# Weight scales and k's column maxima by a GpSimd reduction over partitions, and batch 2's VectorE steps placed behind the splits of w_in

## The chip, the cores and the metric

The kernel runs on one core of a Trainium2 chip. The metric is the device time of one execution in microseconds. The kernel before has a median of 852.67 us over 3 runs (851.4 to 853.17). One further execution was recorded by the hardware profiler; all lines of a profile or trace below are of that one.

## The reference

An attention without a score matrix (q is normalized along its 64 elements, k along its 576 rows) feeds a feed-forward layer of two weights.

```python
# q, k, v: 8 batches x 8 heads x 576 rows x 64; x: 4608 tokens x 512
q_s = np.exp(q - np.max(q, axis=-1, keepdims=True))
q_s = q_s / (np.sum(q_s, axis=-1, keepdims=True) + 1e-09)
k_s = np.exp(k - np.max(k, axis=2, keepdims=True))
k_s = k_s / (np.sum(k_s, axis=2, keepdims=True) + 1e-09)
kv = np.einsum('bhsd,bhse->bhde', k_s, v)
x = np.einsum('bhsd,bhde->bhse', q_s, kv)        # tokens x 512
h = x @ w_in                                     # 512 -> 2048
sp = np.maximum(h, 0.0) + np.log1p(np.exp(-np.abs(h)))
out = (h * erf(sp)) @ w_out                      # 2048 -> 512
```

q, k and v are float32, the two weights are float64.

## The kernel before, in words

**Layout.** A batch has 576 rows: 512 of them lie on 128 partitions (four rows each, two tiles of four heads, `k_0` and `k_1`, `q_0` and `q_1`), the last 64 are a tail (`kt`, `qt`, `vtail`). Two batches form a pair, and a pair's 1152 tokens are three blocks of 384. The feed-forward layer takes a block in four groups of 512 hidden columns: that gives 48 items n, each with a first product (`m`, w_in), the activation (`T`, `G`, `U`) and a second product (`M`, w_out).

**Number formats.** Items 0 to 3 multiply in float32 (L1038, L1116). From item 4 on every operand is split into two float16 parts (hi on ScalarE by `ACTIVATE`, L297; lo on VectorE by `SCALAR_TENSOR_TENSOR`, L298). The first product then uses seven products of sums (`pX`, `pY`, `pZ`, L999), and these need sums of parts of w_in (L322); the second uses three (L1125). The splits scale each group of a weight by a power of two, found from the weight's squares: `wsquares` (Q) collects them on ScalarE, `wscales` (Z, L247 and on) takes the maxima and sets `w_s` (scales), `w_u` (their inverses), `GA`, `GB` and `VW`. `unit` (L1044) makes from `w_u` the factor U of a batch and group for batches 0 and 1.

**Weights.** They arrive as pairs of 32-bit words in sixteen pieces of 1 MB. `wload` issues the first eight through SyncE's queue and the others through GpSimd's:

```python
eng = nc.sync if i < LOADS.count("w") else nc.gpsimd
```

`wdecode` (D, L210 to L216, three VectorE operations for a half piece) turns a piece into float32 and calls `wload` for the next one. A piece's issue waits on its queue for its buffer.

**Maxima of k.** `k_max` (L497 to L501) leaves `kmax`, 128x512, the maxima over each partition's rows. What is still missing is the maximum over partitions. `k_max_T` transposes `kmax` on TensorE (four 128x128, tile `kT` in PSUM) and reduces it on VectorE (`km`, L512); `k_max_rows` transposes `km`'s columns, broadcast, back (`kB` in PSUM). VectorE then subtracts kB from `kt`, `k_0` and `k_1`. The scales of the weights are found in the same manner (`ws_in`, `ws_out`, L259).

**What sets the order.** The text `ORDER` lists the steps of the start and of items 0 to 3; `tok` runs one. Batch 0 has steps of its own in `start` (kmax, kT, kB, qm, ks, ke, qn, kv, ...), where q's second half is subtracted on GpSimd (L871). Batch 1 runs through the generator `attention` and the later ones through `attention16`, one stage at each `A`. From item 4 on a loop lists the steps, `SPLITS` names the weights to split behind an item (S a split, R w_in's sums), and `pace` takes as many `A` as the share of the work done calls for. A scheduler then places the listed operations on each engine's queue, by when it takes their operands to be ready; every engine runs its queue in order. The functions that the change touches:

Of the kernel before, what the change touches and what calls it, by code (L numbers as in the profile page):

```python
# [9 lines left out]
F32 = mybir.dt.float32  # L10
# [23 lines left out]
    kmax qm0 kT kB qe0 qm1 ks2 ks0 ks1 ke2 ke0 ke1 qn0 t0 t1 qe1 qn1 w6 kv0 kn0 kv1 kn1  # L34
# [8 lines left out]
SPLITS = {4: "S2 S3 R3", 5: "S4 S5 R5", 6: "S6", 7: "S7"}  # L43

OUT32 = range(0)
# [12 lines left out]
def attn_moe_kernel(  # L58
# [89 lines left out]
    GB = small[:, 32:36]  # L148
# [100 lines left out]
    def wscales():  # L249


        assert len(wsq) == NJ
        nc.vector.tensor_reduce(small[:, 24:32], sq4, axis=AX.X, op=ALU.max)
        for i, (which, e2) in enumerate((("in", 52), ("out", 50))):

            bk = psh.tile([P, 512], F32, tag="pY" if i == 0 else "pZ", name=f"ws_{which}")
            for g in range(NG):
                o = 24 + 4 * i + g
                nc.tensor.transpose(  # L259
                    bk[:, g * P:(g + 1) * P], small[:, o:o + 1].to_broadcast([P, P]), ident  # L260
                )
            e = at.tile([P, NG], F32, tag="wse", name=f"wse_{which}")
            nc.vector.tensor_reduce(
                e, bk.rearrange("p (g s) -> p g s", g=NG), axis=AX.X, op=ALU.max
            )
            nc.vector.tensor_scalar_max(e, e, TINY)
            nc.vector.tensor_scalar(
                e.bitcast(I32), e.bitcast(I32), 24, 23,
                op0=ALU.logical_shift_right, op1=ALU.logical_shift_left,
            )  # L270
            nc.vector.reciprocal(w_s[which], e)
            nc.vector.tensor_scalar_mul(w_s[which], w_s[which], 2.0**-e2)
            nc.vector.tensor_scalar_mul(w_u[which], e, 2.0**e2)
        wready.add("all")
        m = at.tile([P, 4], F32, tag="wm", bufs=1, name="wm")
        for n, (w, op) in enumerate(
            ((w_s["in"], ALU.min), (w_s["out"], ALU.min),
             (w_u["in"], ALU.max), (w_u["out"], ALU.max))
        ):
            nc.vector.tensor_reduce(m[:, n:n + 1], w, axis=AX.X, op=op)  # L280
        nc.vector.tensor_scalar(
            GA, w_u["out"], m[:, 0:1], m[:, 1:2], op0=ALU.mult, op1=ALU.mult
        )
        nc.vector.scalar_tensor_tensor(
            GA, GA, 2.0**-20, w_u["in"], op0=ALU.mult, op1=ALU.mult
        )
# [4 lines left out]
        nc.vector.tensor_scalar(
            GB, w_u["in"], m[:, 0:1], m[:, 1:2], op0=ALU.mult, op1=ALU.mult
        )
        nc.vector.tensor_scalar_mul(GB, GB, 2.0**-20)

    def split2(src, hi, lo, s):
        nc.scalar.activation(hi, src, AF.Copy, scale=s)  # L297
        nc.vector.scalar_tensor_tensor(lo, src, s, hi, op0=ALU.mult, op1=ALU.subtract)  # L298

    def wsplit(jn):  # L300
# [7 lines left out]
        if which == "out":  # L308
            split2(stg.pop(jn), whalf(jn, 0), whalf(jn, 1), s)
            wdone(jn)  # L310
            return
# [12 lines left out]
    def wsplit_sums(jn):  # L324
        which, g = wjobs[jn]
        sg = stg.pop(jn).rearrange("p (c f) -> p c f", c=4)
        for i in range(2):
            hi, lo = (
                wop(jn, h, 3 + 2 * i, 2).rearrange("p n c f -> p (n c) f") for h in range(2)
            )  # L330
            split2(sg[:, :, 256 * i:256 * i + 256], hi, lo, w_s[which][:, g:g + 1])
        wdone(jn)
# [184 lines left out]
    def k_max_rows(b, km):  # L517

        bk = bank(f"kB_{b}")
        for c in range(NC4):  # L520
            nc.tensor.transpose(
                bk[:, c * P:(c + 1) * P], km[:, c:c + 1].to_broadcast([P, P]), ident
            )
        return bk.rearrange("p (h d) -> p h d", h=H)

# [204 lines left out]
    def attention(b):  # L730
# [96 lines left out]
    def start():  # L827
# [58 lines left out]
        def put(key, val):  # L886
            r[key] = val

        def tc_(c):
# [19 lines left out]
            "kT": ("kmax", lambda: put("km", k_max_T(0, r["kmax"]))),  # L909
            "kB": ("kT", lambda: put("kb", k_max_rows(0, r["km"]))),  # L910
# [162 lines left out]
    def gmul(n):  # L1073
        s, g = st[n], seq[n][2]
        if n < NG:
# [27 lines left out]
    def mm2(n, tt):  # L1103
# [9 lines left out]
        if n < NG or n in OUT32:  # L1113
# [38 lines left out]
    def tok(name):  # L1152
# [71 lines left out]
    for n in range(4, N + 2):  # L1224
# [51 lines left out]
```

## Time and profile before

| | before |
|---|---|
| median of 3 runs | 852.67 us (851.4 to 853.17) |
| the profiled execution | 853.86 us, of which the span (first to last instruction) 851.7 us |
| granted TensorE clock, mean | 0.988 |
| TensorE busy | 811.2 us, 6448 matmuls |
| VectorE busy | 638.2 us, 913 instructions |
| ScalarE busy | 503.0 us, 633 instructions |
| GpSimd busy | 17.6 us, 37 instructions |

PE is TensorE, PEld its weight loads, DVE VectorE, ACT ScalarE, POOL GpSimd, SP SyncE. A row of the timeline has the start in us from the span's start, the duration in us, the engine, the line of the kernel, the operation, the tiles (out<-in) and their size; in brackets stands the time that the engine stood idle before it and what ended this. A row of the windows gives for each stretch of time its length, the busy time of each engine with the number of instructions, the granted clock, the share of time in which the DMA engines were busy, and GB/s.

### The profile page before, as it was taken

The page shows a single profiled execution, that of the slowest core. Times are in us where ns is not written, and L with a number is a line of the kernel's source. Part 1 is how long each engine was busy: PE and PEld are TensorE (multiplying, and loading weights), DVE is VectorE, ACT ScalarE, POOL GpSimd, SP SyncE. Part 2 cuts the span into 40 slices and gives each one's busy share as a digit, 9 for nine tenths or more (in the row PEclk, how much of TensorE's full clock was granted, in tenths as well). Part 3 has the DMA queues.
Part 4 walks back from the last instruction along what each step waited for, and adds up shares of the span by engine and source line. Part 5 has one row for each costly group of instructions (what it writes and reads, how often), then busy time and mean ns, then how long its engine had stood idle before and what let it go on. Part 6 is the DMA issues. An engine that isn't in the chain of part 4 may idle for free.

```text
span 851.7 us, 15370 instructions
## 1 busy us (share of the span) xinstructions
PE 811.2 (95%) x6448; PEld 553.8 (65%) x6448; DVE 638.2 (75%) x913; ACT 503.0 (59%) x633; POOL 17.6 (2%) x37
## 2 busy tenths in 40 slices
PE   2999998899999999999999999999999999999997
PEld 1655557567667667766776676766776676777673
DVE  5999899998997879758865779748866657554543
ACT  2598486777564556555673566555663565543532
POOL 2010000000000000000000000000000000000000
PEclk8899999899999999999999999999999999999999
DMA  9997420016416402412134302322121000100100
GB/s 255 407 250 197 120 75 13 1 25 112 106 35 131 108 9 61 103 31 51 51 70 98 87 14 51 93 51 51 38 51 38 38 2 1 38 1 1 38 1 37
DMA packets 145508, 62.59 MB, mean 73 GB/s; under 512 B 134688, under 2 KB 136736, under 8 KB 145440
## 3 DMA queue, kind: packets, MB, share of 16 engines
q1 hardware_dynamic: 143264, 53.23, 25.1%
q0 software_dynamic: 2176, 8.39, 2.8%
q8 instruction: 50, 0.82, 0.4%
q14 instruction: 18, 0.15, 0.1%
HBM read 45.09 MB, written 9.44 MB: 64 GB/s over the span
## 4 chain that ended last, share of the span: by engine, by line
PE 64%; DVE 19%; ACT 10%; issue 3%; SPq 2%; DMA 1%; ACTq 0%; POOL 0%; DVEq 0%
PE o L1125 27%; PE pX L999 15%; PE pZ L999 7%; ACT G L344 4%; PE o L1116 4%; ACT L344 3%; PE pY L999 3%; DVE G L1079 3%; PE kv L542 2%; DVE H L1097 2%; PE pX L1038 2%; DVE H L1093 2%; SPq L409 2%; PE x L632 1%; DVE wi L298 1%
## 5 line engine op out<-in xcount | busy, mean ns | idle before, releaser
L1125 PE MATMUL o<-wo,H 128*128 128x512 f16 x1584 | 367.0, 380 | 2.8 <-DVE H L1093 1.8
L999 PEld LDWEIGHTS <-wi 128*128 128x128 f16 x3696 | 311.2, 98 | 44.3 <-issue 15.7
L1125 PEld LDWEIGHTS <-H 128*128 128x128 f16 x1584 | 152.7, 98 | 157.4 <-DVE H L1093 2.6
L999 PE MATMUL pX<-x,wi 128*128 128x192 f16 x2112 | 206.2, 248 | 7.6 <-ACT H L1018 4.5
L344 ACT ACT_TABLE_LOAD x104 | 133.4, 1283 | 2.8 <-DVE H L1024 0.8
L1079 DVE SCALAR_TENSOR_TENSOR G<-G,small,H 128x1536 f32<-128x1536 f32 x44 | 79.9, 1817 | 56.2 <-ACT G L344 56.0
L1026 ACT COPY H<-pX 128x384 f32<-128x384 f32 x44 | 20.9, 475 | 165.3 <-PE pX L999 159.9
L999 PE MATMUL pZ<-x,wi 128*128 128x192 f16 x1056 | 104.0, 247 | 3.4 <-ACT x L297 1.8
L344 ACT ACTIVATE G<-H,U 128x768 f32<-128x768 f32 (+1 forms) x60 | 72.7, 1231 | 22.1 <-DVE H L1024 21.5
L1097 DVE TENSOR_TENSOR H<-G,H 128x1536 f16<-128x1536 f32 x44 | 77.2, 1755 | 1.0
L344 ACT ACTIVATE G<-G 128x1536 f32<-128x1536 f32 x48 | 71.2, 1484 | 0.5
L999 PE MATMUL pY<-x,wi 128*128 128x192 f16 x528 | 51.9, 247 | 0.0
L1024 DVE TENSOR_TENSOR H<-pZ,H 128x384 f32<-128x384 f32 x44 | 24.4, 554 | 32.5 <-PE pZ L999 32.1
L1011 DVE COPY H<-pY 128x384 f32<-128x384 f32 x44 | 24.3, 553 | 30.3 <-PE pY L999 30.3
L1116 PE MATMUL o<-wo,G 128*128 128x512 f32 x96 | 43.4, 597 | 0.0
L1093 DVE CAST H<-G 128x1536 f16<-128x1536 f32 x44 | 42.1, 957 | 0.8
L297 ACT ACTIVATE x<-x 128x768 f16<-128x768 f32 (+1 forms) x44 | 32.9, 763 | 12.8 <-DVE x L388 11.1
L1141 DVE TENSOR_SCALAR ob<-o,V 128x512 f32<-128x512 f32 x29 | 21.7, 748 | 24.5 <-PE o L1125 24.5
L298 DVE SCALAR_TENSOR_TENSOR x<-x,x 128x768 f16<-128x768 f32 (+1 forms) x44 | 37.0, 851 | 3.2 <-ACT x L297 3.2
L1013 DVE TENSOR_TENSOR H<-pX,H 128x384 f32<-128x384 f32 x44 | 24.4, 554 | 15.9 <-PE pX L999 15.7
L443 ACT ACTIVATE x<-x 128x384 f32<-128x384 f32 (+1 forms) x52 | 17.5, 394 | 30.0 <-PE x L632 27.4
L1116 PEld LDWEIGHTS o<-wo,G 128*128 128x128 f32 x96 | 17.5, 190 | 18.7 <-issue 18.2
(184 smaller groups left out, 762.7 us busy)
## 6 DMA issues: line engine op xcount, KB each, us to landing
out_dram<-ob SPq DMA_DIRECT2D x32, 256.0 KB, 2.4
vbuf<-in_v_dram SPq DMA_DIRECT2D x60, 128.0 KB, 3.1
q<-in_q_dram SPq DMA_DIRECT2D x56, 128.0 KB, 3.4
k<-in_k_dram SPq DMA_DIRECT2D x56, 128.0 KB, 3.1
wo<-in_moe_w_in_dram SPq DMA_DIRECT2D x4, 1024.0 KB, 17.2
wi<-in_moe_w_out_dram POOLq DMA_DIRECT2D x2, 1024.0 KB, 8.9
wi<-in_moe_w_in_dram SPq DMA_DIRECT2D x2, 1024.0 KB, 9.4
raw<-in_moe_w_out_dram POOLq DMA_DIRECT2D x2, 1024.0 KB, 8.0
```

The lines of the kernel that those rows point to most:

```text
L297: nc.scalar.activation(hi, src, AF.Copy, scale=s)
L298: nc.vector.scalar_tensor_tensor(lo, src, s, hi, op0=ALU.mult, op1=ALU.subtract)
L344: i = nc.scalar.activation(out_, in_, func, **kw)
L999: nc.tensor.matmul(o, w[wl][:, c, a * P:(a + 1) * P], x[:, xl, xi, c, :], start=(new and a == 0 and c == 0 and i == 0), stop=(c == 1 and i ...
L1011: nc.vector.tensor_copy(C[0, 0], bank2("Y"))
L1013: add(C[0, 0], bank2("X"), C[0, 0], op=ALU.add)
L1024: add(C[0, 1], bank2("Z"), C[0, 1], op=ALU.add)
L1079: nc.vector.scalar_tensor_tensor(flat(s["G"]), flat(s["G"]), (GB if n in OUT32 else GA)[:, g:g + 1], flat(s["H"]), op0=ALU.mult, op1=ALU.mult,
L1093: nc.vector.tensor_copy(flat(s["gh"]), flat(s["G"]))
L1097: nc.vector.tensor_tensor(flat(s["gl"]), flat(s["G"]), flat(s["gh"]), op=ALU.subtract)
L1116: nc.tensor.matmul(o, s["G"][:, a, ts_], w[:, a, :], start=(first_ and a == 0), stop=(last_ and a == FG - 1),)
L1125: nc.tensor.matmul(o, s[gt][:, a, ts_], w[wl][:, a, :], start=(first_ and a == 0 and i == 0), stop=(last_ and a == FG - 1 and i == 2),)
```

## The change

- **k's maxima of batches 0 and 1.** `k_max_all` takes the place of `k_max_T` and `k_max_rows`: one `partition_all_reduce` on GpSimd takes `kmax` (128x512) and leaves in every partition of `kB`, now an SBUF tile, the maximum over the partitions. Later batches keep the way over TensorE. In `ORDER` the steps kT and kB become one, kB, directly behind kmax.
- **The weights' scales.** `wscales` takes the eight columns of both weights through one `partition_all_reduce` (128x8), and computes scales and inverses of both at once. `GB` goes; `unit` makes the four factors of a batch in one operation.
- **The order behind the splits.** `wsplit` keeps in `wlast` the last lo split of the latest group of w_in; attention's stages and the splits of w_out are issued behind that instruction (`tc.issue_after`). In `SPLITS` the splits of w_out come behind those of w_in.
- `OUT32`, which was empty, and the branches that asked for it are gone.

```diff
 ORDER = """
-    kmax qm0 kT kB qe0 qm1 ks2 ks0 ks1 ke2 ke0 ke1 qn0 t0 t1 qe1 qn1 w6 kv0 kn0 kv1 kn1
+    kmax kB qm0 qe0 qm1 ks2 ks0 ks1 ke2 ke0 ke1 qn0 t0 t1 qe1 qn1 w6 kv0 kn0 kv1 kn1
...
-SPLITS = {4: "S2 S3 R3", 5: "S4 S5 R5", 6: "S6", 7: "S7"}
+SPLITS = {4: "S3 R3 S2", 5: "S5 R5 S4", 6: "S6", 7: "S7"}
...
         nc.vector.tensor_reduce(small[:, 24:32], sq4, axis=AX.X, op=ALU.max)
-        for i, (which, e2) in enumerate((("in", 52), ("out", 50))):
-
-            bk = psh.tile([P, 512], F32, tag="pY" if i == 0 else "pZ", name=f"ws_{which}")
-            for g in range(NG):
...
-            nc.vector.tensor_scalar_mul(w_u[which], e, 2.0**e2)
+        e = small[:, 32:40]
+        nc.gpsimd.partition_all_reduce(e, small[:, 24:32], P, bass_isa.ReduceOp.max)
+        nc.vector.tensor_scalar_max(e, e, TINY)
+        nc.vector.tensor_scalar(
+            e.bitcast(I32), e.bitcast(I32), 24, 23,
+            op0=ALU.logical_shift_right, op1=ALU.logical_shift_left,
+        )
+        nc.vector.tensor_scalar_mul(w_u["in"], e[:, :NG], 2.0**52)
+        nc.vector.tensor_scalar_mul(w_u["out"], e[:, NG:], 2.0**50)
+        nc.vector.reciprocal(small[:, 4:12], small[:, 12:20])
...
-        for n, (w, op) in enumerate(
-            ((w_s["in"], ALU.min), (w_s["out"], ALU.min),
-             (w_u["in"], ALU.max), (w_u["out"], ALU.max))
-        ):
-            nc.vector.tensor_reduce(m[:, n:n + 1], w, axis=AX.X, op=op)
+        for n, (c, op) in enumerate(((4, ALU.min), (12, ALU.max))):
+            nc.vector.tensor_reduce(
+                m[:, 2 * n:2 * n + 2], small[:, c:c + 8].rearrange("p (w g) -> p w g", w=2),
+                axis=AX.X, op=op,
+            )
...
+    wlast = [None]
+
+    def behind(ins):
+
+        return tc.issue_after(ins) if ins is not None else nullcontext()
...
         if which == "out":
-            split2(stg.pop(jn), whalf(jn, 0), whalf(jn, 1), s)
+            with behind(wlast[0]):
+                split2(stg.pop(jn), whalf(jn, 0), whalf(jn, 1), s)
...
-            split2(sg[:, :, 256 * i:256 * i + 256], hi, lo, w_s[which][:, g:g + 1])
+            r = split2(sg[:, :, 256 * i:256 * i + 256], hi, lo, w_s[which][:, g:g + 1])
+        wlast[0] = r.ins
...
+    def k_max_all(b, kmax):
+
+        kb = at.tile([P, DM], F32, tag="qT", name=f"kB_{b}")
+        nc.gpsimd.partition_all_reduce(kb, hd(kmax), P, bass_isa.ReduceOp.max)
+        return kb.rearrange("p (h d) -> p h d", h=H)
...
-        km = k_max_T(b, kmax)
+        kb = k_max_all(b, kmax)
         q_sub(rows(qs[0]), 16, f"q_{b}_0")
         yield SHARES[1]
-        kb = k_max_rows(b, km)
...
-            "kT": ("kmax", lambda: put("km", k_max_T(0, r["kmax"]))),
-            "kB": ("kT", lambda: put("kb", k_max_rows(0, r["km"]))),
+            "kB": ("kmax", lambda: put("kb", k_max_all(0, r["kmax"]))),
...
-        if b < 2 and (b, g) not in udone:
-            udone.add((b, g))
-            nc.vector.tensor_tensor(U, w_u["in"][:, g:g + 1], bat[b]["ux"], op=ALU.mult)
+        if b < 2 and b not in udone:
+            udone.add(b)
+            nc.vector.tensor_scalar_mul(bat[b]["U"], w_u["in"], bat[b]["ux"])
...
         if c == "A":
-            r = next(att, None)
+            with behind(wlast[0]):
+                r = next(att, None)
```

Three places show what the scheduler makes of it. First GpSimd's queue at the start. Before, behind the memsets of v's tail, it holds the issue of a piece of w_out (the buffer `wi_89`), q's second half and more issues:

```order
L433 MEMSET vtail 64x520
L434 MEMSET vtail 64x8
L189 DMA wi_89<-in_moe_w_out_dram 128x2x1024
L871 TENSOR_TENSOR q_1_136<-G_raw_1_109,q_1_m 128x1024
L433 MEMSET vtail 64x520
L434 MEMSET vtail 64x8
L189 DMA raw_359<-in_moe_w_out_dram 128x2x1024
L189 DMA wo_95<-in_moe_w_in_dram 128x2x1024
```

In the changed kernel the reduction stands there, between two `ISA` rows without operands (each loads a GpSimd library: the one for the reduction, then the one from before):

```order
L425 MEMSET vtail 64x520
L426 MEMSET vtail 64x8
L521 ISA
L521 ISA kB_146<-kmax_139 128x512
L868 ISA
L868 TENSOR_TENSOR q_1_136<-G_raw_1_109,q_1_m 128x1024
L425 MEMSET vtail 64x520
L426 MEMSET vtail 64x8
L188 DMA wi_89<-in_moe_w_out_dram 128x2x1024
L188 DMA raw_349<-in_moe_w_out_dram 128x2x1024
```

The issue of `wi_89` has moved from ahead of q's subtraction to behind it and behind the memset of the second v tail.

Second, VectorE's queue at the start, behind the last step of kmax. Before, `km` and q's maxima, then k's subtractions ahead of q's norm (`q_0_r`, L461 to L467):

```order
L501 TENSOR_TENSOR kmax_139<-kmax_139,kt_105 64x512
L512 TENSOR_REDUCE km_154<-kT_149 128x4
L870 TENSOR_REDUCE q_0_m<-H_raw_q 128x16
L857 TENSOR_TENSOR kt_105<-kt_105,kB_156 64x512
L871 TENSOR_TENSOR q_0_135<-H_raw_q,q_0_m 128x1024
L859 TENSOR_TENSOR k_0_133<-H_raw_0_101,kB_156 128x1024
L870 TENSOR_REDUCE q_1_m<-G_raw_1_109 128x16
L859 TENSOR_TENSOR k_1_134<-H_raw_1_103,kB_156 128x1024
L461 TENSOR_REDUCE q_0_r<-q_0_135 128x16
L463 TENSOR_SCALAR q_0_r<-q_0_r 128x16
L466 RECIPROCAL q_0_r<-q_0_r 128x16
L467 TENSOR_TENSOR q_0_135<-q_0_135,q_0_r 128x1024
```

And in the changed kernel:

```order
L493 TENSOR_TENSOR kmax_139<-kmax_139,kt_105 64x512
L867 TENSOR_REDUCE q_0_m<-H_raw_q 128x16
L868 TENSOR_TENSOR q_0_135<-H_raw_q,q_0_m 128x1024
L867 TENSOR_REDUCE q_1_m<-G_raw_1_109 128x16
L453 TENSOR_REDUCE q_0_r<-q_0_135 128x16
L455 TENSOR_SCALAR q_0_r<-q_0_r 128x16
L458 RECIPROCAL q_0_r<-q_0_r 128x16
L459 TENSOR_TENSOR q_0_135<-q_0_135,q_0_r 128x1024
L854 TENSOR_TENSOR kt_105<-kt_105,kB_146 64x512
L856 TENSOR_TENSOR k_0_133<-H_raw_0_101,kB_146 128x1024
L856 TENSOR_TENSOR k_1_134<-H_raw_1_103,kB_146 128x1024
```

`km` is gone, q's second maxima and the norm of q's first half stand ahead of k's three subtractions, and the norm of q's second half (`q_1_r`), which stood right behind the rows of before, has moved behind the first decodes of w_in, beyond these rows.

Third, VectorE's queue in the stretch where w_in's group 3 (`wi_91`, `wi_92`) is split and items 4 and 5 take their first products (`H_895` and `H_1011`, in the changed kernel `H_853` and `H_969`). Before, steps of batch 2 (`kmax_1177` and the subtraction on `q_0_800`) stand among the splits:

```order
L298 SCALAR_TENSOR_TENSOR wi_90<-wi_91,small,wi_90 128x1024
L1021 TENSOR_TENSOR H_895<-pX_910,H_895 128x2x192
L1011 COPY H_1011<-pY_1012 128x2x192
L498 TENSOR_TENSOR kmax_1177<-k_2_1178 128x256
L298 SCALAR_TENSOR_TENSOR wi_91<-wi_92,small,wi_91 128x1024
L298 SCALAR_TENSOR_TENSOR wi_91<-wi_92,small,wi_91 128x512
L501 TENSOR_TENSOR kmax_1177<-kmax_1177,kt_602 64x512
L322 TENSOR_TENSOR wi_92<-wi_92 128x2x256
L1013 TENSOR_TENSOR H_1011<-pX_1026,H_1011 128x2x192
L322 TENSOR_TENSOR wi_92<-wi_92 128x2x256
L455 TENSOR_TENSOR q_0_800<-q_0_800,q_0_m 128x1024
L322 TENSOR_TENSOR wi_92<-wi_92 128x2x256
```

In the changed kernel the same stretch holds splits, and one of w_out (`wo_97`):

```order
L282 SCALAR_TENSOR_TENSOR wi_91<-wi_92,small,wi_91 128x1024
L282 SCALAR_TENSOR_TENSOR wi_91<-wi_92,small,wi_91 128x512
L1020 TENSOR_TENSOR H_853<-pZ_882,H_853 128x2x192
L313 TENSOR_TENSOR wi_92<-wi_92 128x2x256
L1017 TENSOR_TENSOR H_853<-pX_868,H_853 128x2x192
L313 TENSOR_TENSOR wi_92<-wi_92 128x2x256
L1007 COPY H_969<-pY_970 128x2x192
L313 TENSOR_TENSOR wi_92<-wi_92 128x2x256 x2
L282 SCALAR_TENSOR_TENSOR wi_91<-wi_92,small,wi_91 128x1024
L282 SCALAR_TENSOR_TENSOR wo_97<-wo_93,small,wo_97 128x2048
L282 SCALAR_TENSOR_TENSOR wi_91<-wi_92,small,wi_91 128x1024
L1009 TENSOR_TENSOR H_969<-pX_984,H_969 128x2x192
```

Batch 2's maxima now come behind the last split of the last group of w_in (`wi_92` from `sg_594`), among the splits of x's next block (`x_2`):

```order
L282 SCALAR_TENSOR_TENSOR wo_93<-wo_94,small,wo_93 128x2048
L1087 CAST H_969<-G_1080 128x1536
L282 SCALAR_TENSOR_TENSOR x_2_1115<-x_749,x_2_1115 128x768
L282 SCALAR_TENSOR_TENSOR x_2_1115<-x_749,x_2_1115 128x384
L489 TENSOR_TENSOR k_2_1134<-k_0_572 128x512
L1091 TENSOR_TENSOR H_969<-G_1080,H_969 128x1536
L490 TENSOR_TENSOR kmax_1133<-k_2_1134 128x256
L380 TENSOR_TENSOR x_749<-x_749 128x2x192
L489 TENSOR_TENSOR k_2_1134<-k_1_577 128x512
L380 TENSOR_TENSOR x_749<-x_749 128x2x192
L490 TENSOR_TENSOR kmax_1133<-k_2_1134 128x256
L380 TENSOR_TENSOR x_749<-x_749 128x2x192
```

So `kmax` of batch 2, which before lay between the splits of w_in, has moved behind all of them.

More of the change, by code (lines that the diff above doesn't have):

```diff
@@ L1 @@
-from contextlib import ExitStack
+from contextlib import ExitStack, nullcontext
 import concourse.bass as bass
 import concourse.tile as tile
+from concourse import bass_isa
 from concourse import mybir
@@ L41 @@
 """
-SPLITS = {4: "S2 S3 R3", 5: "S4 S5 R5", 6: "S6", 7: "S7"}
-OUT32 = range(0)
+SPLITS = {4: "S3 R3 S2", 5: "S5 R5 S4", 6: "S6", 7: "S7"}
 OUTS = [0, 1, 2, 3]
@@ L147, in attn_moe_kernel @@
     GA = small[:, 20:24]
-    GB = small[:, 32:36]
     wjobs = JOBS
@@ L253, in wscales @@
         nc.vector.tensor_reduce(small[:, 24:32], sq4, axis=AX.X, op=ALU.max)
-        for i, (which, e2) in enumerate((("in", 52), ("out", 50))):
-            bk = psh.tile([P, 512], F32, tag="pY" if i == 0 else "pZ", name=f"ws_{which}")
-            for g in range(NG):
[L258 to L272, printed above, removed]
-            nc.vector.tensor_scalar_mul(w_u[which], e, 2.0**e2)
+        e = small[:, 32:40]
[8 more added lines that the diff above has]
+        nc.vector.reciprocal(small[:, 4:12], small[:, 12:20])
         wready.add("all")
         m = at.tile([P, 4], F32, tag="wm", bufs=1, name="wm")
-        for n, (w, op) in enumerate(
-            ((w_s["in"], ALU.min), (w_s["out"], ALU.min),
-             (w_u["in"], ALU.max), (w_u["out"], ALU.max))
-        ):
-            nc.vector.tensor_reduce(m[:, n:n + 1], w, axis=AX.X, op=op)
+        for n, (c, op) in enumerate(((4, ALU.min), (12, ALU.max))):
[3 more added lines that the diff above has]
+            )
         nc.vector.tensor_scalar(
@@ L289, in wscales @@
         )
[L291 to L294, printed above, removed]
     def split2(src, hi, lo, s):
         nc.scalar.activation(hi, src, AF.Copy, scale=s)
-        nc.vector.scalar_tensor_tensor(lo, src, s, hi, op0=ALU.mult, op1=ALU.subtract)
+        return nc.vector.scalar_tensor_tensor(lo, src, s, hi, op0=ALU.mult, op1=ALU.subtract)
+    wlast = [None]
+    def behind(ins):
+        return tc.issue_after(ins) if ins is not None else nullcontext()
     def wsplit(jn):
@@ L1079, in gmul @@
         nc.vector.scalar_tensor_tensor(
-            flat(s["G"]), flat(s["G"]), (GB if n in OUT32 else GA)[:, g:g + 1], flat(s["H"]),
+            flat(s["G"]), flat(s["G"]), GA[:, g:g + 1], flat(s["H"]),
             op0=ALU.mult, op1=ALU.mult,
         )
-        if n in OUT32:
-            return
         hl = flat(s["H"]).bitcast(F16)
@@ L1112, in mm2 @@
         ts_ = slice(tt * P, (tt + 1) * P)
-        if n < NG or n in OUT32:
+        if n < NG:
             w = stg[jn].rearrange("p (a e) -> p a e", a=FG)
@@ L1230, in attn_moe_kernel @@
                 tok(f"m{n}.{i}")
-            if 4 < n <= N and i < 2 and n - 1 not in OUT32:
+            if 4 < n <= N and i < 2:
                 tok(f"{'IO'[i]}{n - 1}")
```

## The prediction

> **What bounds the kernel now.** The page first: its busy line, the forty slices and the chain.
>
> ```profile
> span 851.7 us, 15370 instructions
> PE 811.2 (95%) x6448; PEld 553.8 (65%) x6448; DVE 638.2 (75%) x913; ACT 503.0 (59%) x633; POOL 17.6 (2%) x37
> ...
> PE   2999998899999999999999999999999999999997
> ...
> DVE  5999899998997879758865779748866657554543
> ...
> PE 64%; DVE 19%; ACT 10%; issue 3%; SPq 2%; DMA 1%; ACTq 0%; POOL 0%; DVEq 0%
> ```
>
> TensorE carries the span, with VectorE as the second limit, and VectorE's digits are high only in the first third. All edits fall in the first 260 us. From there on both programs have VectorE's instructions in the same order, and a lead or a loss made before is carried to the end. So I read the early stages one by one, in windows of ten microseconds.
>
> ```profile
> core 0: us, PE busy (x) PEld busy (x) DVE busy (x) ACT busy (x) POOL busy (x), PEclk, DMA share, GB/s
> 30.00:40.00 10.00, 10.00 (x32) 5.39 (x31) 9.93 (x22) 6.67 (x20) 0.00 (x0) 1.00 1.02 408
> ...
> 90.00:100.00 10.00, 10.00 (x35) 5.99 (x34) 9.84 (x18) 4.22 (x12) 1.12 (x1) 1.00 0.44 142
> ...
> 130.00:140.00 10.00, 6.94 (x60) 6.08 (x58) 9.62 (x14) 4.89 (x8) 0.00 (x0) 0.83 0.07 27
> 140.00:150.00 10.00, 7.86 (x89) 7.29 (x87) 9.51 (x14) 8.59 (x11) 0.00 (x0) 1.00 0.01 2
> 150.00:160.00 10.00, 6.76 (x39) 4.92 (x39) 9.66 (x11) 6.18 (x7) 0.00 (x0) 0.66 0.00 0
> ...
> 180.00:190.00 10.00, 9.94 (x101) 6.54 (x100) 10.00 (x11) 6.47 (x9) 0.00 (x0) 1.00 0.21 49
> ```
>
> Three regimes show. From 30 to 100 us TensorE and VectorE are both full. From 130 to 160 VectorE is still full at 9.5 to 9.7 of 10, but TensorE is busy 21.56 of 30: it waits 8.44 us for w_in's splits, and its granted clock falls to a mean of 0.66. From 165 on both are full again. So work taken from either full engine counts, and what is only put off on VectorE comes back later.
>
> **Part 1, the start (0 to 30 us).** The maxima of k for batch 0 leave TensorE for GpSimd, and VectorE takes q's steps ahead of k's.
>
> ```profile
> 3.85 0.84 POOL L189 DMA_DIRECT2D wi<-in_moe_w_out_dram  x1
> ...
> 8.20 0.68 DVE L501 TENSOR_TENSOR kmax<-kmax,kt 64x512 f32<-64x512 f32 x1 [0.54 <-DMA kt<-in_k_dram]
> ...
> 12.77 1.22 DVE L870 TENSOR_REDUCE q_m<-H_raw_q 128x16 f32<-128x1024 f32 x1 [1.93 <-DMA H_raw_q<-in_q_dram]
> ...
> 18.12 1.90 POOL L871 TENSOR_TENSOR q<-G_raw,q_m 128x1024 f32<-128x1024 f32 x1 [13.44 <-DMA v<-in_v_dram]
> ...
> 20.06 1.06 ACT L866 ACTIVATE q<-q 128x1024 f32<-128x1024 f32 x1 [2.12 <-POOL q L871]
> ...
> 26.51 0.16 DVE L561 TENSOR_SCALAR rd<-kv 128x2 f32<-128x2 f32 x1 [1.45 <-PE kv L542]
> ```
>
> Two things matter. First a transfer moves. GpSimd's queue used to issue 1 MB of w_out at 3.85. In the changed order this issue stands behind the reduction, q's subtraction and the second vtail memset, and this memset waits for the kv products, so it goes out only after about 23 us. Today this megabyte shares the full DMA engines with q's first half:
>
> ```profile
> 8.00:12.00 4.00, 2.97 (x13) 2.30 (x14) 1.38 (x2) 0.00 (x0) 0.00 (x0) 1.00 1.05 377
> ...
> wi<-in_moe_w_out_dram POOLq DMA_DIRECT2D x1, 1024.0 KB, 9.2
> H_raw_q<-in_q_dram SPq DMA_DIRECT2D x1, 512.0 KB, 9.5
> ```
>
> It lands at 3.85 + 9.2 = 13.05, q's half when VectorE's wait for it ends, 12.77. At 377 GB/s, 1.05 MB is 2.8 us; nearly all of it lies ahead of q, so q lands some 2.5 us earlier, and v and the weight pieces behind it in SyncE's queue likewise. VectorE starts q's maxima at 12.77 for this reason alone, and until 26.51 it stands still only 1.45 us more. So, if nobody else holds it, this stretch ends 2.5 us earlier. I take **-2.5** (bounds 0 and -2.8).
>
> Second, GpSimd gets a series: load a library, reduce, load the standard library again, subtract q's second half (1.90), and only then can ScalarE take q's exponential (1.06). The trace shows neither a library load nor such a reduction, so both are bounded. The load L: the program of before holds one such instruction too, between a memset that ends at 1.88 and the AFFINE_SELECT at 1.92, which puts the low end at 0.04; the high end is the 9.2 of a 1 MB transfer on the same full engines. [...] The reduction X of 128x512: at least one pass over 512 elements, half of the 1.90 of the 1024-element subtraction, so 0.95; at most seven such passes (128 partitions in halving steps), 6.65; I take the middle, 3.8.
>
> GpSimd is free at 4.0 (issue row above), so k's maxima are there at max(8.88, 4.0 + 4.6) + 3.8 = 12.7. VectorE wants them behind q's first half: 10.3 + two reductions of 1.22, the subtraction (1.21) and the norm (a reduction and a product like these and two small operations, 2.8) = 16.7. Free, with 4 us to spare. q's second half: 12.7 + 4.6 + 1.9 + 1.06 = 20.3. Today VectorE ends this stretch at 26.51; less the 2.5 of the transfer and less the norm of q's second half (2.8), which now stands behind the first decodes, that is 21.2, and kv's norm with those decodes (some ten short steps of 0.16 to 0.69) adds about 4 by my estimate. So VectorE wants q's second half at some 25.2. Free again, as long as 2L + X stays under 25.2 - 4.0 - 1.9 - 1.06 = 18.2; beyond that VectorE stands still for the excess. So **0** from the centre, up to 7 us lost with both high ends (2 x 9.2 + 6.65 = 25.1, 6.9 over). [...]
>
> **Part 2, batch 1 (60 to 80 us).** Both engines are full here.
>
> ```profile
> 62.87 0.71 POOL L189 DMA_DIRECT2D wi<-in_moe_w_out_dram  x1 [2.15 <-DVE wo L216]
> ...
> 68.48 0.69 DVE L501 TENSOR_TENSOR kmax<-kmax,kt 64x512 f32<-64x512 f32 x1
> 69.23 0.66 PE L508 MATMUL kT<-ident,kmax 128*128 128x128 f32 x4
> 70.34 0.68 DVE L512 TENSOR_REDUCE km<-kT 128x4 f32<-128x512 f32 x1
> 71.08 0.65 PE L521 MATMUL kB<-ident,km 128*128 128x128 f32 x4
> ```
>
> Removed: 0.66 + 0.65 of TensorE and 0.68 of VectorE. The load starts behind the issue at 62.87 and ends at 68.2 with the central L; kmax ends at 69.17, and the reduction at 73. The order puts thirteen steps (decodes and q's norm, 0.2 to 1.2 each) between kmax and k's subtraction, some 12 us by the rows of their kind, so it stands near 79 to 81 and 6 us cover the reduction; without that cover each further microsecond of X stalls VectorE. **TensorE -1.3, VectorE -0.7.**
>
> **Part 3, the scales (109 to 114 us).**
>
> ```profile
> 108.82 0.19 DVE L253 TENSOR_REDUCE small<-sq 128x8 f32<-128x32 f32 x1
> 109.06 0.65 PE L259 MATMUL ws_in<-ident,small 128*128 128x128 f32 x4
> 109.55 0.60 PE L259 MATMUL ws_out<-ident,small 128*128 128x128 f32 x4
> ...
> 112.44 1.78 ACT L297 ACTIVATE wi<-wi,small 128x1024 f16<-128x1024 f32 x2
> ...
> 113.64 1.95 DVE L298 SCALAR_TENSOR_TENSOR wi<-wi,small,wi 128x1024 f16<-128x1024 f32 x2
> ```
>
> From the reduction's end (109.01) to the first split on ScalarE are 3.4 us; VectorE's first own split is at 113.64. Changed: one GpSimd reduction of 8 elements (the library is still loaded), then six small operations at about 0.15 each on one path, the two reductions and GA behind them. An 8-element reduction is bounded by GpSimd's small memset (0.10, the row below) and by seven of these with a hand-over, 1.5; I take 1.0. Then the split starts 1.0 + 0.2 + 0.9 = 2.1 us after the reduction, 1.3 us earlier. On VectorE an own split could start at 109.01 + 1.0 + 0.9 + 0.3 (GA) + 1.2 (waiting for ScalarE's first half of the pair) = 112.4, with an x split (0.95) done in the gap that used to come later; against 113.64 that is 1.2 + 0.95 = 2.2. I take **VectorE -2** and **TensorE -1.25** (the transposes). The memset of kvbd ahead of it on GpSimd waits for the tail product, but this product now stands far earlier in TensorE's order, so I cost it at nothing.
>
> ```profile
> L434 POOL MEMSET vtail<- 64x8 f32 x8 | 0.8, 106 | 0.4
> ```
>
> **Part 4, batch 2 behind the splits (126 to 220 us).**
>
> ```profile
> 122.96 2.35 DVE L298 SCALAR_TENSOR_TENSOR wo<-wo,small,wo 128x2048 f16<-128x2048 f32 x1
> ...
> 126.42 0.69 DVE L497 TENSOR_TENSOR k<-k 128x512 f32<-128x512 f32 x1
> 127.02 1.21 DVE L454 TENSOR_REDUCE q_m<-q 128x16 f32<-128x1024 f32 x1
> 129.09 0.42 DVE L498 TENSOR_TENSOR kmax<-k 128x256 f32<-128x256 f32 x1
> ...
> 147.24 1.21 DVE L455 TENSOR_TENSOR q<-q,q_m 128x1024 f32<-128x1024 f32 x1
> ...
> 152.79 2.08 PE L999 MATMUL pX<-x,wi 128*128 128x192 f16 x12 [4.19 <-ACT H L1018]
> ...
> 161.45 0.68 DVE L512 TENSOR_REDUCE km<-kT 128x4 f32<-128x512 f32 x1
> ...
> 219.86 0.81 PE L632 MATMUL x<-q,kvbd 128*128 128x512 f16 x3 [0.91 <-issue]
> ```
>
> Eight steps of batch 2 leave the split stage: kmax (two of 0.69, two of 0.42, one of 0.69), q's maxima and subtraction (1.21 each), km (0.68), 6.0 us by the rows of their kind, and one w_out split (2.35): 8.3 us. That is about TensorE's wait there. But batch 2's x product (219.86) needs those 6.0 us, and between 160 and 200 VectorE has no room (10.00 of 10 in the row above). So TensorE, which keeps its order, runs ahead and then stands before batch 2's first products. I count this part as **0** for the last limit, which is VectorE's chain up to batch 3; the bounds are -8.4 (nothing given back) and +4 (k's subtraction of batch 2 comes that much later against TensorE).
>
> **The sum.** VectorE: -2.5 - 0.7 - 2 = -5.2. TensorE: -2.5 - 1.3 - 1.25 = -5.05. Both limits move by the same 5 us, so whichever ends last, about -5. The profiled execution took 853.86 (span 851.7); 853.86 - 5 = 848.9. The median of the three runs is 852.67, 1.2 below the profiled one, and less 5 is 847.7. I say 848.
>
> **The rivals.**
>
> *The loads in series (slower).* For: GpSimd was free at the start, now it has two loads and a reduction ahead of q's second half, and the DMA engines are over full there (1.05). Against: by central values 2L + X is 13.0, which leaves 18.2 - 13.0 = 5.2 us of cover. With both high ends VectorE first waits 3 us for k's maxima (13.2 + 6.65 = 19.9 against 16.7), then for q: 7 us in all, 848 + 7 = 855. It turns slower than before once 2L + X exceeds 18.2 + 5 = 23.2.
>
> [...]
>
> *Given back (no change).* VectorE stays full to 220, the start's 2.5 us are eaten by a load, and TensorE stands before batch 2. Left is 848 + 2.5 + 2 = 852.5.
>
> *TensorE keeps it (much faster).* If batch 2's chain has slack that I don't see, the 8.4 us of the split stage stay: 848 - 7 = 841. Against: TensorE already waits 0.91 at 219.86.
>
> **How the numbers follow.** About 0.2% (1.7 us) is what a measurement of this kernel can tell from no change. Forecast (842 to 851) 0.57, much faster 0.12, given back 0.13, loads in series 0.12, partition walk 0.06. Faster: 0.57 + 0.12 and a little of the third, 0.70. Same 0.12, slower 0.18. The range runs from the fastest rival to a little above the loads in series, 840 to 857; what it leaves out is the walk and the ends, some 0.12.
>
> **What would show it.** q's maxima on VectorE near 10.3 with no wait on GpSimd before 26; the first pX of w_in some 2.5 us earlier; no VectorE wait on GpSimd at k's subtraction of batch 1; the first split on ScalarE about 2 us after the reduction of the squares; TensorE's idle time in the split stage shrunk, and more of it just before batch 2's kv and x products. It would be wrong if a wait of VectorE or ScalarE on GpSimd over 3 us stood in the first 35 us, or if TensorE's idle in the split stage vanished without returning.

## The result and the profile after

The changed kernel takes 874.12 us (median of 4 runs, 872.49 to 878.16) against 852.14 us: 2.6% slower, ratio 1.0264, 95% interval 1.0227 to 1.0301. The prediction said 848 and a range to 857. The page of the changed kernel, its busy line, three rows of the forty slices and the chain (this execution took 878.16 us, 4 above the median, so what is read from it comes out a little larger than the 22 us between the medians):

```profile
span 876.4 us, 15319 instructions
PE 816.5 (93%) x6424; PEld 553.1 (63%) x6424; DVE 635.2 (72%) x894; ACT 504.6 (58%) x634; POOL 23.8 (3%) x40
...
PE   2499999798999999999999999999999999999997
...
DVE  4499978798889697866895597856884665644553
ACT  1288696847467556735765457636756456453632
...
PE 42%; DVE 30%; ACT 16%; issue 4%; DMA 3%; SPq 1%; POOL 0%; ACTq 0%; DVEq 0%
```

Work was removed: 24 matmuls and 19 VectorE instructions fewer stand in the records, and VectorE is busy 3.0 us less. TensorE's share still falls from 95% to 93%, and the chain that ended last runs for 30% through VectorE instead of 19%. Two places show it: the first two slices (2 and 4 tenths, before 2 and 9), and slices 8 and 10 (7 and 8 tenths, before 8 and 9, between 153 and 219 us).

**The start.** GpSimd's timeline, with the idle time ahead of each operation in brackets:

```profile
0.93 0.95 POOL L107 MEMSET kvbd<- 128x1024 f16 x1
12.43 1.21 POOL masks.py:199 TENSOR_SCALAR_AFFINE_SELECT ident<-ident 128x128 f32<-128x128 f32 x1 [10.54 <-issue]
...
15.25 0.10 POOL L426 MEMSET vtail<- 64x8 f32 x1
24.21 1.80 POOL L521 PARTITION_ALL_REDUCE kB<-kmax  x1 [8.86 <-issue]
38.09 1.89 POOL L868 TENSOR_TENSOR q<-G_raw,q_m 128x1024 f32<-128x1024 f32 x1 [12.08 <-issue]
...
87.93 2.90 POOL L521 PARTITION_ALL_REDUCE kB<-kmax  x1 [7.30 <-DVE q L459]
...
122.79 0.39 POOL L254 PARTITION_ALL_REDUCE small<-small  x1 [5.96 <-DVE small L252]
```

"issue" is a wait for nothing that the profile shows. It stands exactly where the order has an `ISA` row without operands: ahead of the identity's select, of the reduction and of q's subtraction, and a fourth time ahead of batch 1's reduction, where the page names a step that happened to end then. No row and no view shows a load itself: where this document gives a load a time, it is the length of such a gap. Three of them in a row, 10.5 + 8.9 + 12.1 = 31.5 us, now stand in front of q's second half. VectorE's timeline shows who waits:

```profile
11.01 1.22 DVE L867 TENSOR_REDUCE q_m<-H_raw_q 128x16 f32<-128x1024 f32 x1 [1.51 <-DMA H_raw_q<-in_q_dram]
...
26.05 0.68 DVE L854 TENSOR_TENSOR kt<-kt,kB 64x512 f32<-64x512 f32 x1 [8.43 <-POOL kB L521]
...
31.49 0.16 DVE L559 TENSOR_SCALAR rd<-kv 128x2 f32<-128x2 f32 x1 [2.49 <-PE kv L540]
...
41.10 1.22 DVE L453 TENSOR_REDUCE q_r<-q 128x16 f32<-128x1024 f32 x1 [4.81 <-ACT q L863]
```

VectorE stands still 8.43 us for k's maxima and 4.81 for q's second half. Batch 0's `rd`, at 26.51 before, comes at 31.49.

**How far each item is behind.** The scaled G of an item (L1079 before, L1075 after) is one VectorE instruction for each item from 4 on. Its start after less its start before, in us:

```
item              4     5     6     7     8     9    10    11    12    13 ...  last
after           10.7   6.2  20.1  20.4  21.9  17.2  21.3  25.2  22.5  22.8     24.7
```

Some 11 us are lost by item 4, 4.5 are won back by item 5, and 13.9 are lost between items 5 and 6, where batch 2's steps now stand. So there are two losses, one on each side of item 5. They are tested apart.

### The profile page after: what moved, and what is told of

The parts are those of the page before. It is cut to its first block, busy times and chain, and to the rows that moved or that the text cites. A ratio compares the mean times of both kernels' runs of the same rounds, so it can differ in the third digit from the quotient of the medians.

```text
span 876.4 us, 15319 instructions
## 1 busy us (share of the span) xinstructions
PE 816.5 (93%) x6424; PEld 553.1 (63%) x6424; DVE 635.2 (72%) x894; ACT 504.6 (58%) x634; POOL 23.8 (3%) x40
## 4 chain that ended last, share of the span: by engine, by line
PE 42%; DVE 30%; ACT 16%; issue 4%; DMA 3%; SPq 1%; POOL 0%; ACTq 0%; DVEq 0%
PE o L1119 20%; PE pX L995 11%; ACT G L336 7%; ACT L336 6%; PE pZ L995 5%; DVE G L1075 4%; DVE H L1091 3%; PE pY L995 2%; DVE H L1087 2%; DVE x L282 2%; PE x L630 2%; PE kv L540 1%; DVE x L380 1%; DVE wi L282 1%; DMA q<-in_q_dram 1%
## 5 line engine op out<-in xcount | busy, mean ns | idle before, releaser
L1075 DVE SCALAR_TENSOR_TENSOR G<-G,small,H 128x1536 f32<-128x1536 f32 x44 | 80.0, 1817 | 67.8 <-ACT G L336 67.8
L336 ACT ACTIVATE G<-H,U 128x768 f32<-128x768 f32 (+1 forms) x60 | 72.7, 1231 | 22.1 <-DVE H L1020 21.5
L281 ACT ACTIVATE x<-x 128x768 f16<-128x768 f32 (+1 forms) x44 | 32.7, 762 | 27.3 <-DVE x L380 25.8
L540 PE MATMUL kv<-vbuf,k 128*64 128x65 f32 x480 | 22.1, 231 | 9.5 <-ACT k L863 9.3
```

Source lines behind the costliest of these rows:

```text
L336: i = nc.scalar.activation(out_, in_, func, **kw)
L540: nc.tensor.matmul(bk[a * D:(a + 1) * D, c * W:(c + 1) * W], kk, vv, start=(t == 0), stop=(t == TM),)
L1075: nc.vector.scalar_tensor_tensor(flat(s["G"]), flat(s["G"]), GA[:, g:g + 1], flat(s["H"]), op0=ALU.mult, op1=ALU.mult,)
```

## The experiments

All kernels were timed beside the kernel before; a ratio is to its runs on the same chip. "Left over", "order", "batch 0" and so on are explained below.

| run | what it is | median, us | ratio (95%) |
|---|---|---|---|
| e1 | before + order part | 861.34 | 1.0103 (1.0083 to 1.0123) |
| e2 | after - order part | 865.91 | 1.0156 (1.0135 to 1.0176) |
| e3 | after + library back | 864.13 | 1.0143 (1.0112 to 1.0175) |
| e4 | after, batch 0 over TensorE | 863.49 | 1.0129 (1.0110 to 1.0149) |
| e5 | after - order + library back | 855.32 | 1.0017 (1.0003 to 1.0032) |
| e6 | before + order of attention's steps alone | 857.34 | 1.0053 (1.0031 to 1.0076) |
| e7 | before + k's maxima alone, library back | 857.18 | 1.0056 (1.0033 to 1.0078) |
| e8 | e5, batch 0 over TensorE | 857.15 | 1.0039 (1.0021 to 1.0058) |
| e9 | before + scales alone, library back | 854.71 | 1.0026 (1.0012 to 1.0040) |
| e10 | before + order of w_out's splits alone | 854.19 | 1.0025 (1.0007 to 1.0042) |
| e12 | e5, q's second half on VectorE | 853.56 | 1.0005 (0.9990 to 1.0019) |
| e13 | e12, batch 1 over TensorE | 855.81 | 1.0027 (1.0006 to 1.0049) |
| e14 | e1, behind w_in's group 2 only | 855.77 | 1.0032 (1.0007 to 1.0058) |
| e15 | before + a library left over | 855.28 | 1.0023 (1.0007 to 1.0039) |

**e1 and e2: the order part, put in and taken out.**

```diff
-SPLITS = {4: "S2 S3 R3", 5: "S4 S5 R5", 6: "S6", 7: "S7"}
+SPLITS = {4: "S3 R3 S2", 5: "S5 R5 S4", 6: "S6", 7: "S7"}
...
-            r = next(att, None)
+            with behind(wlast[0]):
+                r = next(att, None)
```

(for e1 with `behind`, `wlast` and the same around w_out's splits; e2 is the reverse on the changed kernel)

> The kernel before with the order part alone (the split order and the issue of attention's stages and w_out's splits behind w_in's). In the changed kernel item 4's scaled G is 10.7 us late, item 5's 6.2, item 6's 20.1, and the end 24.7. Theory A (the order part itself costs what is lost behind item 5): 860 to 867, item 5's G no later than before, item 6's some 10 or more late. Theory B (all comes from GpSimd's loads at the start): 849 to 855, within 3 of before.

> The changed kernel without the order part. Theory A (order costs 12 to 16 by itself): 858 to 863, and item 6's G only some 6 to 10 us late. Theory B (the loads cost it all): 872 to 876. Three long gaps before GpSimd's first operations (10.5, 8.9, 12.1 us) stay in both.

Theory A holds in both directions: 1.0% in the one kernel, 1.1% in the other. Item 5's G is 6.2 earlier in e1 and item 6's 7.7 later (10 or more was expected), a loss of 13.9, as in the changed kernel. e2 came out 3 us above A's range, with item 6's G 14.5 late instead of 6 to 10: item 4 is 10.9 late, and without the order part item 5 wins back only 1.7 of it. All the rest, 1.6%, is not the order.

**e3: the library back.** One addition on four columns, behind the scales.

```diff
+        nc.gpsimd.tensor_tensor(small[:, 40:44], GA, GA, op=ALU.add)
```

> The changed kernel with one GpSimd addition on four columns behind the weights' scales, which makes GpSimd load the standard library again at some 123 us. Theory C (the 10.5 us before the identity's select are a load that is needed because the execution before left the other library in place): the select starts near 2 us as before, the two other gaps stay, and the time falls by 6 to 10, to 864 to 868. Rival D (a program with two libraries pays it at its first use in any case, or the gap is the late arrival of code): the gap stays and the time is 873 to 876.

Theory C: the ratio falls from 1.0264 to 1.0143, some 10 us. GpSimd's timeline of e3:

```profile
2.17 0.29 POOL masks.py:199 TENSOR_SCALAR_AFFINE_SELECT ident<-ident 128x128 f32<-128x128 f32 x1 [0.29 <-POOL kvbd L107]
...
13.02 1.96 POOL L522 PARTITION_ALL_REDUCE kB<-kmax  x1 [8.85 <-DMA G_raw<-in_q_dram]
24.27 2.08 POOL L869 TENSOR_TENSOR q<-G_raw,q_m 128x1024 f32<-128x1024 f32 x1 [9.29 <-DVE wi L209]
...
118.46 0.95 POOL L279 TENSOR_TENSOR small<-small 128x4 f32<-128x4 f32 x1 [7.67 <-DVE wi L314]
```

The select is at 2.17 again (1.92 before), and a gap of 7.67 us has appeared at 110 to 118, where nobody waits for GpSimd. Nothing ahead of the select was changed. So the 10.5 us come from the execution before; my reading, which e15 tests from the other side, is that it ended with the other library in place.

**e4: batch 0's maxima over TensorE in the changed kernel.**

```diff
-    kmax kB qm0 qe0 qm1 ks2 ks0 ks1 ke2 ke0 ke1 qn0 t0 t1 qe1 qn1 w6 kv0 kn0 kv1 kn1
+    kmax qm0 kT kB qe0 qm1 ks2 ks0 ks1 ke2 ke0 ke1 qn0 t0 t1 qe1 qn1 w6 kv0 kn0 kv1 kn1
```

> The changed kernel with batch 0's maxima over TensorE as before (batch 1's and the scales stay on GpSimd). Two of the three gaps at the start go (8.9 and 12.1); the first one (10.5 before the select) stays, and now k's transposes wait for the identity until 13.7 instead of 9.5. If the loads at the start cost 8 to 10 in all: 865 to 869. If they cost all 22: 853 to 858. If they are hidden: 873 to 876.

863.49, a little below the first case. The select still waits (12.15), but TensorE's transposes only move from 9.03 to 12.48, and item 4's G is 0.4 early. What is left of the loss is the order part again (items 5 to 6: 12.4).

**e5: both causes undone.** The edits of e2 and e3 together.

> The changed kernel without the order part and with the standard library loaded back behind the scales: both findings of the first set undone at once. If they add up (10.0 for the load left over, 8.2 to 8.9 for the order), 855 to 857, some 3.5 above before, which is then what the two loads between the start's steps still cost. If the order part only costs where the start is late, 862 to 865.

They add up: 855.32, ratio 1.0017. The two causes are all but 0.2% of the 2.6%.

**e6, e10 and e14: what the order part loses.** e6 keeps only `behind` around attention's steps, e10 only the w_out half of the part. e14 is e1 with the wait moved one group forward:

```diff
-        wlast[0] = r.ins
+        if jn != wjobs.index(("in", 3)):
+            wlast[0] = r.ins
```

> The kernel before with only attention's stages issued behind w_in's last split; the order in SPLITS and the issue of w_out's splits stay as before. Theory A1 (the loss of 8.9 comes from batch 2's steps being put off): 859 to 862, item 6's scaled G near 187. Theory A2 (it comes from the w_out splits' place): 850 to 854, item 6's G near 179.

> The kernel before with the other half of the order part: w_out's splits issued behind w_in's last split and listed behind them, attention's stages as before. Attention's half cost 4.5 (ratio 1.0053), both 8.8 (1.0103). If the two add up: ratio 1.004 to 1.006, 857 to 859. If they only cost together: 852 to 855.

> As e1 (the kernel before with the order part alone), but batch 2's steps and w_out's splits wait only for the splits of w_in's group 2, so that they may stand between the splits of group 3 again. Theory F (the order part loses because VectorE has nothing to fill its waits in the split stage and batch 2's steps then stand ahead of item 6's products): ratio 1.000 to 1.005, item 6's scaled G within 3 of before, VectorE's busy time from 120 to 200 above 76. Rival G (any delay of batch 2's maxima costs as much): ratio 1.008 to 1.012 as e1.

e6 lies between its two cases, and e10 in the second of its own. The halves cost 0.5% and 0.3%, less than the 1.0% of both; the intervals are too wide to say that the rest arises only with both. e14 gets two thirds of the loss back, with item 6's G at +1.3 (its item 4 is at -2.0), as theory F has it. Rival G is out: batch 2's transposes `kT` still come at 170.09 in e14, against 148.00 before and 177.27 in e1, and most of the loss is gone. The windows of the 80 us from 120 on, of before, e1, e14 and e6 in this order:

```profile
120.00:200.00 80.00, 70.92 (x590) 50.96 (x590) 78.28 (x102) 62.31 (x73) 1.59 (x3) 0.94 0.12 32
```

```profile
120.00:200.00 80.00, 67.64 (x531) 46.42 (x530) 73.66 (x89) 55.53 (x65) 0.96 (x1) 0.94 0.09 24
```

```profile
120.00:200.00 80.00, 69.22 (x587) 49.38 (x586) 76.03 (x96) 58.70 (x69) 1.59 (x3) 0.96 0.12 32
```

```profile
120.00:200.00 80.00, 67.22 (x571) 49.22 (x570) 77.08 (x101) 57.62 (x68) 1.59 (x3) 0.94 0.10 28
```

VectorE (the third busy time) is busy 78.28, 73.66, 76.03 and 77.08. In e1 it has nothing else to do while it waits for ScalarE (3.1 us for G, 1.5 for the hi halves of w_in's splits, 1.2 for H; before, 0.9 in all), and 4.6 us of its time are lost. But e6 has lost only 1.2 us of VectorE's time and still takes 0.5% more, so the lost fill is not the whole. The second effect is the block itself. Between item 5's G and item 6's, VectorE's queue in e1 holds nine steps of batch 2 (7.2 us by their rows) and two splits of w_out (4.7); before, one step of batch 2 stands there (1.2). Item 6 needs none of batch 2, but its own steps stand behind the block, and the engines wait for each other in turn. ScalarE's timeline of e1 shows it:

```profile
174.99 0.84 ACT L297 ACTIVATE x<-x 128x768 f16<-128x768 f32 x1 [5.15 <-DVE x L396]
...
180.19 0.48 ACT L1034 COPY H<-pX 128x384 f32<-128x384 f32 x1 [3.30 <-PE pX L1007]
```

In the 19 us that end with item 6's G, the windows of before (160 to 179) and of e1 (168 to 187) have:

```profile
160.00:179.00 19.00, 18.44 (x154) 13.16 (x152) 18.50 (x23) 17.23 (x19) 0.00 (x0) 1.00 0.00 1
```

```profile
168.00:187.00 19.00, 15.95 (x107) 9.75 (x106) 17.46 (x24) 10.28 (x11) 0.00 (x0) 0.91 0.00 1
```

ScalarE falls from 17.23 to 10.28, TensorE from 18.44 to 15.95 and its granted clock from 1.00 to 0.91, while VectorE stays busy. e14 changes the fill and the block together, so how much of the 9 us each of the two effects takes is not shown.

**e15: a library left over, alone.** The kernel before with one reduction behind the scales, so that the execution ends with the other library.

```diff
+        nc.gpsimd.partition_all_reduce(small[:, 40:44], GB, P, bass_isa.ReduceOp.max)
```

> The kernel before with one reduction of four columns on GpSimd behind the scales, whose result nobody reads, and nothing that loads the standard library back. If the library stays from one execution to the next, the identity's select starts near 12 instead of 2 although nothing in the program ahead of it has changed, and k's transposes at 12.5 instead of 9.0 as in e4, with VectorE's first decode stage 1.5 late. Time: by e4 (item 4's G no later than before) 852 to 855, ratio under 1.004, so the same load that cost 10 in the changed kernel costs little where no other load is queued behind it. Rival: it costs its 10 here too, 861 to 864.

GpSimd's timeline and TensorE's of e15:

```profile
12.21 0.28 POOL masks.py:199 TENSOR_SCALAR_AFFINE_SELECT ident<-ident 128x128 f32<-128x128 f32 x1 [10.31 <-issue]
```

```profile
12.54 1.12 PE L510 MATMUL kT<-ident,kmax 128*128 128x128 f32 x4 [12.54 <-POOL ident masks.py:199]
```

The gap of 10.3 appears in a program whose start is the same as before, which settles where it comes from. It costs only 0.2% here: the transposes are 3.5 late, and `rd` 1.4. The same load costs 10 us where two more loads and a reduction are queued behind it on GpSimd.

**e7, e8, e9, e12, e13: what the useful parts are worth without the two losses.** e7, e8 and e9 put parts on GpSimd alone, with the library loaded back behind the scales; e12 takes q's second half off GpSimd, so that one library serves from batch 0 to the scales (the gap ahead of batch 1's reduction is 7.31 in e5 and 0.77 in e12):

```diff
-            (nc.gpsimd if hf else nc.vector).tensor_tensor(
+            nc.vector.tensor_tensor(
```

e13 is e12 with `k_max_T` and `k_max_rows` for batch 1.

> The kernel before with k's maxima of batches 0 and 1 on GpSimd alone (scales over TensorE, order as before), and the standard library loaded back behind the scales. Against e5 it tells what the scales' reduction is worth: if it saves 2 to 3 as the prediction has it, 857 to 860; if nothing, as e5, 855 to 857.

> Batch 1's maxima and the scales on GpSimd, the standard library loaded back, batch 0 over TensorE, order as before. No load is left at the start. If the start's two loads cost 3 to 4 and the rest gains the 2 to 3.5 that the prediction counts: 848 to 851, faster than before by 0.2 to 0.5%. If batch 1's load (7.3 us before its reduction) costs what the scales gain: 851 to 854.

> The scales' reduction alone on GpSimd; k's maxima of batches 0 and 1 over TensorE and the order as before; the library is loaded by a one-column reduction behind the last early weight issue (near 64 us) and the standard one loaded back behind the scales. By e5 against e7 the scales' part is worth 3 to 4: theory S says 849 to 851 beside a before of 853. If that difference came from how VectorE's other steps fell, 852 to 856.

> The changed kernel without the order part, with the standard library loaded back at the scales, and q's second half subtracted on VectorE, so that GpSimd needs no standard library between batch 0's reduction and the scales. Two loads go (q's wait of 11.3 and batch 1's of 7.3); VectorE gets 1.2 more. If loads on the path cost what e5 has over a kernel with no load: 850 to 853, batch 1's reduction right behind its kmax or the issue ahead of it. If the loads are hidden in e5 by now: 855 to 857.

> As e12, but batch 1's maxima over TensorE as before. Tells what batch 1's reduction is worth when no load stands before it. By the prediction's price (1.3 of TensorE, 0.7 of VectorE): 1 to 2 slower than e12. If batch 1's part is a loss in itself (e8 against e5 hints at it): 2 to 5 faster.

e8 missed both of its cases, and e9 fell into the second: both are slower than before where a gain was hoped for. None of the five beats the kernel before; e12, between its two cases, comes nearest, equal to it within its interval. e13 against e12 (1.0027 to 1.0005, medians 2.2 us apart) hints that batch 1's reduction is a small gain when no load stands before it, but the intervals overlap. e7 against e5 gives the scales 3.3 us by the ratios and 1.9 by the medians, while the scales alone (e9) lose 2.2: this is not settled. One explanation that no run here tests is that with every such edit the splits behind it fall in another order.

In e12 the start is early, and it doesn't last. VectorE's `rd`, TensorE's kv of batch 1 and GpSimd at the scales:

```profile
23.73 0.16 DVE L560 TENSOR_SCALAR rd<-kv 128x2 f32<-128x2 f32 x1 [0.86 <-PE kv L541]
```

```profile
74.68 0.69 PE L541 MATMUL kv<-vbuf,k 128*64 128x65 f32 x16 [2.11 <-ACT k L337]
```

```profile
109.27 0.95 POOL L589 MEMSET kvbd<- 128x1024 f16 x1 [14.39 <-PE xt L628]
110.20 0.40 POOL L254 PARTITION_ALL_REDUCE small<-small  x1
```

`rd` is 2.8 earlier than before, though only 0.9 to 1.3 earlier than in e6, e10 and e14 (24.98, 24.74, 24.60), whose start is that of the kernel before. At 74.68 TensorE waits 2.11 us for k of batch 1, which it did not before, and item 4's G is only 0.8 early. At the scales the reduction takes 0.40, but it stands behind a memset that waits for TensorE: the squares' maxima are there at 108.83, the reduction starts at 110.20.

## Why the prediction was wrong

- **The bound: held.** What the changed kernel loses comes as idle time of TensorE and VectorE, in the start and in the split stage, the places that the prediction named.
- **The transfer (-2.5): not shown.** q's maxima start at 11.01 in the changed kernel and at 10.50 in e12, against 12.77 before and 10.3 forecast. That looks like the gain, but e6, e10 and e14 have the start of the kernel before, with the issue of w_out at 3.85, and there they start at 10.44 to 10.68 too. In e10:

```profile
10.44 1.21 DVE L878 TENSOR_REDUCE q_m<-H_raw_q 128x16 f32<-128x1024 f32 x1
...
H_raw_q<-in_q_dram SPq DMA_DIRECT2D x1, 512.0 KB, 6.2
```

q's first half takes 6.1 to 6.3 us to land in these three executions and 9.5 in that of before, so the 12.77 was not the fixed price of the old order. What there is of a gain the loads eat in the changed kernel, and in e12 it is mostly gone by item 4 (0.8).
- **The loads ("Free again, as long as 2L + X stays under" 18.2): the step that failed first.** Two errors in one term. The number: the `ISA` row that stood 0.04 behind a memset was taken for the low end of a load's price, but there, as I read e3 and e15, nothing had to be loaded. In the changed kernel this same row stands in a gap of 10.54 us, so there are three loads, not two. The size: L was put at 4.6, the middle of its bounds 0.04 and 9.2; no run shows a load of 4.6 (the shortest, in e15, is 6.58), and at the start it measured 8.9 and 12.1. The reduction X was put at 3.8 and took 1.8. So 2L + X was 22.7, 4.5 over the cover. The chances also give 0.06 to a walk over the partitions, which no run shows: the two reductions of 128x512 took 1.80 and 2.90 in the changed kernel. The third load, which no term held, put the other two some 11 us back and made the 8.43 us wait for k's maxima, well over the 3 us in the first 35 that the prediction had named as a sign of being wrong. The cover itself was counted right, as e5 shows, where no third load stands at the start:

```profile
28.74 1.22 DVE L454 TENSOR_REDUCE q_r<-q 128x16 f32<-128x1024 f32 x1 [2.96 <-ACT q L864]
```

VectorE wants q's second half at 25.8 there (25.2 forecast), k's maxima cost no wait, and 2L + X is 21.5. That the changed kernel's wait of 4.81 also fits the 4.5 is in part luck, since both queues had moved by some 11 us. "Loads in series" was the right rival with one load too few: with two loads e5 takes 855.32 (ratio 1.0017), with the third e2 takes 865.91 (1.0156).
- **Batch 1: half right.** The reduction came late (87.93, 7.6 behind the end of kmax at 80.34), and k's subtraction, 12.0 behind that end, did not wait for it, as counted. The gain of 1.3 and 0.7 is not shown: e12 is no faster than before, and the 2.2 us that it has over e13 are not clear of the noise.
- **The scales (-2 on VectorE): not confirmed.** The step itself is as forecast where nothing stands before the reduction: 0.39 for the reduction, and in the changed kernel ScalarE's first split starts 1.7 us after the squares' maxima do (3.6 before). As time it is not seen (e9). The memset of kvbd "at nothing" was wrong in e12, where the reduction starts 1.4 after the maxima are there (0.2 in e8) and VectorE's first split is no earlier than before (113.59 against 113.64).
- **Batch 2 behind the splits ("0", bounds -8.4 and +4): the step that failed second.** TensorE does run ahead (item 5's G 6.2 early in e1), but it does not then stand where the prediction had it, before batch 2's first products: in e1 and in the changed kernel these start with no wait over 0.3 us (in e14, whose loss is a third, there is one of 2.5). It stands before item 6 and what follows (item 6's G 7.7 late), because batch 2's steps and w_out's splits stand ahead of that item in VectorE's queue. The sum of zero became a loss of 9 us, over twice the bound: the bound priced the delay of k's subtraction alone, neither VectorE's lost fill nor the items that queue behind the block. Nor were the 8.44 us of TensorE's idle time waits for w_in's splits alone: 4.19 of them, in a row that the prediction shows, are one wait for ScalarE's copy of H. The 0.66 given there as the mean clock is one window's; the mean of the three rows is 0.83.
- **The sum.** The ratios multiply nearly: 1.012 for the load left over (after against e3), 1.011 for the order (after against e2), 1.002 for all the rest (e5). The forecast -5 is, without the two losses, between +0.2% and no change.

## What to carry to other kernels

Before an operation of a second GpSimd library is put into a kernel, count the loads in GpSimd's queue, the one between the end of an execution and the start of the next included, and put each where nobody waits for GpSimd for as long as a load took here, 6.6 to 12.1 us. In this kernel the steps of batch 2 stood in the waits of a nearly full VectorE (78.28 of 80 us busy before); gathered behind the splits, in e1, they stood ahead of item 6, and its G came 7.7 us later. Before a shift of 2 us in one trace is called a gain, look how far the same row moves in other runs that leave it alone (here from 12.77 to 10.44). A row of before that costs nothing (0.04 here, 10.54 in the changed kernel) shows that its condition was met, not that the operation is cheap.

## What was not expected of the hardware

The longest gaps stand where the DMA share is 0.96 or more. Windows over gaps of the changed kernel, the three at the start and the one of batch 1 (the last two numbers are DMA share and GB/s):

```profile
2.00:12.40 10.40, 0.00 (x0) 0.00 (x0) 4.27 (x7) 0.03 (x1) 0.00 (x0) 1.00 1.04 265
15.40:24.20 8.80, 2.97 (x13) 1.99 (x11) 2.12 (x4) 0.00 (x0) 0.00 (x0) 1.00 1.00 356
26.00:38.00 12.00, 7.91 (x86) 5.61 (x86) 7.22 (x16) 4.08 (x6) 0.01 (x1) 1.00 1.03 402
80.70:87.90 7.20, 7.20 (x23) 4.18 (x22) 7.20 (x10) 4.72 (x14) 0.00 (x0) 1.00 0.39 146
```

With a DMA share of 1.00 to 1.04 these loads took 8.9 to 12.1 us, at 0.39 the load took 7.3, and the loads back of e3 and e12 behind the scales took 7.7 and 7.2. In windows over the gaps of e3 and e5 the loads of the first 40 us took 8.4 (at a share of 1.21), 8.9 (1.07), 9.3 (0.96) and 11.3 (1.03), the later ones 6.9 (0.34), 7.3 (0.40), 7.7 (0.30) and 7.8 (0.36). So it is no steady rise with the share, and that the transfers are the cause is not shown. The shortest gap is 6.58 (e15). The reduction over partitions was cheap instead: 1.8 to 2.9 us for 128x512 and 0.4 for 128x8 (0.8 for the 128x4 of e15), where the prediction had put 3.8 and 1.0.
